# Retention plus low-rank mixer on one core: the start of the kernel put in another order, for its loads, its first two batches and the first chunks of the third

## The chip, the cores and the metric

The kernel runs on one core of a Trainium2 chip. The metric is the device time of one execution in microseconds. Before the change it is 326.08 us, the median of 13 runs (325.36 to 326.92).

## The reference

Eight batches of eight heads, 576 positions, 64 features to a head. Retention comes first, then a mixer over positions of rank 32, then a two-layer perceptron with a residual:

```python
scores = scale * np.matmul(q, k.transpose(0, 1, 3, 2))
ret = scores * Dmat[None]                 # gamma_h ** (row - col), 0 above the diagonal
x = np.matmul(ret, v)                     # heads side by side: x is (8, 576, 512)
h = x.transpose(0, 2, 1) @ U @ V          # U (576, 32), V (32, 576)
u = x + h.transpose(0, 2, 1)
out = u + np.maximum(u @ w_ch1, 0.0) @ w_ch2     # 512 -> 2048 -> 512
```

Inputs and output are float32 in HBM; the kernel multiplies in bfloat16.

## The kernel before

**Two kinds of attention.** The batches go in pairs. For batches 2 to 7 the rows of a pair are nine chunks of 128 (`order`, L576): four of the even batch, one that holds the last 64 rows of one batch and the first 64 of the other, four of the odd batch. A chunk is loaded from q, k and v (`load`, L235, three tiles of 256 KB), cast and scaled to bf16 (`cast_chunk`, L254: the aligned half of k and all of q on ACT in L261 and L264, the rest of k on DVE in L263, v on GpSimd in L272), and transposed by a DMA on SyncE's queue (`xbar`, L276). `prep` is cast and transpose. `section` (L387) then makes scores, the running state and the result on TensorE; its first matmuls (L296) need the transposed chunk.

Batches 0 and 1 are done by a start written out by hand. Their rows are four units of 256 rows (numbers 0 and 1 in batch 0, 2 and 3 in batch 1) and two half chunks J (0: the last 64 rows of batch 0; 1: the first 64 of batch 1). A unit is loaded as six tiles (`load_u`, L605, issued in L617: k, q and v in two halves of heads each), scaled or cast on GpSimd (`scale_u`, L637; `cast_u`, L630), transposed on TensorE against an identity (`T_u`, L646, copies in L664 to L669), scored (`SC_u`, L675), masked on DVE (`mask_u`, L690), multiplied by v (`RV_u`, L701) and by the state before it (`QS_u`, L744), summed into the state (`ST_u`, L760, put in bf16 by `Sblk`, L770), and scaled into x (`XS_u`, L752). The half chunks have the same steps with a J in the name; `cast_J` (L799) casts k and q, `prep_vJ` (L814) scales v on GpSimd. `warm` (L205) issues matmuls on the identity whose result nobody reads.

**Mixer and perceptron.** `mixer_items` (L417) gives MA (x times U), MH (times V, plus x, which is u; added on DVE in L464) and MT (u transposed: on TensorE with a copy on ACT in L489 for the first pair, by DMA for the others). `y1_items` (L504) is the first layer, sixteen times four matmuls (L515) and a Relu on ACT (L520) for each stretch of columns; the second half of the first pair is split into 384 and 256 columns. `y2_items` (L531) is the second layer (L549) and the store. PSUM has three buffers of the tag "big"; the Y1 results, the T_u transposes and the Y2 sums take turns in them, so each waits for the copy out of the tile three places before.

**What sets the order.** Each engine works through its instructions in the order of the program, and there is no scheduler (`tc.manual_schedule()`). `startup` (L909) does batch 0 up to the first transposed u; `first_stretch` (L1033) interleaves batch 1 with the sixteen Y1 items of batch 0 (`y(n)` emits the next n), then both mixers of the pair and the first Y1 stretches of batch 1 (`Y1(f, seg)`). `merge` (L20) then lays the rest of Y1 and Y2 against the sections of batch 2 at given fractions of the work, with `fetch(n)` (load) and `ready(n)` (prep) of chunk n of the pair at others. Later batches have the same merge with other lists.

**Loads.** q, k and v come on SyncE's queue, with the DMA transposes; U and V too (`load_u_rows`, L177). The weights come on GpSimd's queue with a cast to bf16: w1 in pieces of columns (`load_w1`, L212, of which f counts blocks of 128 columns), w2 in eight pieces of two row blocks (`load_w2`, L217). A load's issue waits in its queue until its buffer has been read; the staging pool has fifteen buffers (L70), used in turn. Unit 3's loads have a gate: GpSimd writes one element of the tile first (L615), so the issue waits for GpSimd to get there. The first w2 load waits likewise for a DVE write (L1089).

## Time and profile before

| what | value |
|---|---|
| median of 13 runs | 326.08 us |
| the profiled execution | 326.03 us, span 324.3 us |
| TensorE matmul busy | 311.2 us (96%) |
| ACT, DVE, GpSimd busy | 146.0, 172.0, 101.3 us |
| first Y1 matmul (L515) | 24.47 us |
| first Y2 matmul (L549) | 73.70 us |
| last matmul's end | 321.3 us |
| granted TensorE clock | 1.0 all along |
| loads of q, k, v in full tiles | 4.8 to 5.5 us from issue to landing (median) |
| w1 and w2 pieces of 256 KB | 8.4 us (median of 14) |

A timeline row gives the start and the length in us, engine, line, operation, what it writes and reads, the shape, how many instructions were merged, and in brackets the idle time of the engine before the row with what ended it. A q behind an engine's name (SPq) is its sequencer: it issues a transfer. The DMA share is the mean busy share of sixteen DMA engines; transfers overlap in them, so that it can go over 1. Durations of single matmuls hold the pipe's latency; from start to start a 512-column matmul takes 0.216 us.

### The profile page before, as it was taken

The page shows a single profiled execution, that of the slowest core. Times are in us where ns is not written, and L with a number is a line of the kernel's source. Part 1 is how long each engine was busy: PE and PEld are TensorE (multiplying, and loading weights), DVE is VectorE, ACT ScalarE, POOL GpSimd, SP SyncE. Part 2 cuts the span into 40 slices and gives each one's busy share as a digit, 9 for nine tenths or more (in the row PEclk, how much of TensorE's full clock was granted, in tenths as well). Part 3 has the DMA queues.
Part 4 walks back from the last instruction along what each step waited for, and adds up shares of the span by engine and source line. Part 5 has one row for each costly group of instructions (what it writes and reads, how often), then busy time and mean ns, then how long its engine had stood idle before and what let it go on. Part 6 is the DMA issues. An engine that isn't in the chain of part 4 may idle for free.

```text
span 324.3 us, 9118 instructions
## 1 busy us (share of the span) xinstructions
PE 311.2 (96%) x3860; PEld 171.2 (53%) x3885; DVE 172.0 (53%) x342; ACT 146.0 (45%) x334; POOL 101.3 (31%) x172
## 2 busy tenths in 40 slices
PE   7999989989999999999999999999999999999996
PEld 3575545755444444457644454457644444467544
DVE  7866546228635577456744477555844475500012
ACT  5857547892020484058800474058700572047400
POOL 7697239223113732142221523051321500010000
PEclk9999999999999999999999999999999999999999
DMA  7999999999965999969998599859998440330022
GB/s 211 257 239 260 235 191 195 205 169 144 260 167 128 240 196 202 206 138 191 189 192 174 142 185 209 212 141 158 189 212 183 107 68 3 105 107 0 2 78 84
DMA packets 152904, 53.30 MB, mean 164 GB/s; under 512 B 132032, under 2 KB 150336, under 8 KB 152864
## 3 DMA queue, kind: packets, MB, share of 16 engines
q1 hardware_dynamic: 144512, 40.40, 67.8%
q0 software_dynamic: 8352, 12.32, 15.6%
q8 instruction: 30, 0.49, 0.7%
q14 instruction: 10, 0.08, 0.1%
HBM read 36.85 MB, written 9.44 MB: 143 GB/s over the span
## 4 chain that ended last, share of the span: by engine, by line
PE 71%; DMA 5%; ACT 3%; DVE 3%; issue 2%; SPq 1%; DVEq 0%
PE ps_y L549 32%; PE ps_y L515 31%; DMA qkT<-qk 3%; PE pp L296 2%; DVE u L464 2%; DMA uT<-u 1%; ACT y L520 1%; PE pp L316 1%; PE pp L328 1%; PE ps_y L560 1%; DMA stage_t<-in_q_dram 1%; PE AB L358 1%; PE ph L458 1%; PE pa L431 1%; ACT s_sb L373 1%
## 5 line engine op out<-in xcount | busy, mean ns | idle before, releaser
L515 PE MATMUL ps_y<-uT,w_sb 128*128 128x256 bf16 (+2 forms) x768 | 133.1, 326 | 1.7 <-ACT y L520 1.0
L520 ACT ACTIVATE y<-ps_y 128x384 bf16<-128x384 f32 (+2 forms) x192 | 89.6, 491 | 96.7 <-PE ps_y L515 95.9
L549 PE MATMUL ps_y<-w_sb,y 128*128 128x512 bf16 x535 | 123.8, 379 | 2.2 <-issue 1.1
L515 PEld LDWEIGHTS <-w_sb 128*128 128x128 bf16 x768 | 72.3, 98 | 49.5 <-issue 3.3
L549 PEld LDWEIGHTS <-y 128*128 128x128 bf16 x560 | 52.6, 98 | 61.1
L272 POOL TENSOR_TENSOR vt<-stage_t,vscale 64x256 bf16<-64x256 f32 (+1 forms) x81 | 50.1, 619 | 63.0 <-DMA stage_t<-in_v_dram 45.0
L538 DVE TENSOR_TENSOR o_sb<-ps_y,u 128x512 f32<-128x512 f32 (+2 forms) x38 | 25.2, 664 | 82.4 <-PE ps_y L549 80.1
L541 POOL DMA_DIRECT2D out_dram<-o_sb x31 | 17.1, 553 | 105.4 <-DVE o_sb L538 101.6
L304 DVE TENSOR_TENSOR ret<-pp,triH 128x512 bf16<-128x512 f32 x27 | 18.7, 691 | 24.2 <-PE pp L328 18.7
L464 DVE TENSOR_TENSOR u<-ph,xt 128x768 bf16<-128x768 f32 (+2 forms) x24 | 21.8, 950 | 5.9 <-PE ph L458 4.2
L437 ACT ACTIVATE a_sb<-pa 128x128 bf16<-128x128 f32 x8 | 2.2, 278 | 43.3 <-PE pa L431 43.3
L344 DVE TENSOR_TENSOR xt<-pp,qscale 128x512 bf16<-128x512 f32 x27 | 18.6, 689 | 4.7 <-PE pp L328 4.2
L338 DVE COPY q<-qkT 64x256 bf16<-64x256 bf16 x48 | 13.2, 275 | 14.6 <-DMA qkT<-qk 13.6
L383 DVE TENSOR_TENSOR s_sb<-AB,Af 64x256 bf16<-64x256 f32 x42 | 17.7, 422 | 2.1 <-ACT s_sb L378 1.5
L263 DVE CAST qk<-stage_t 64x256 bf16<-64x256 f32 x54 | 18.1, 335 | 1.2
L264 ACT ACTIVATE qk<-stage_t 128x512 bf16<-128x512 f32 x27 | 16.8, 621 | 0.4 <-DMA stage_t<-in_q_dram 0.4
L635 POOL CAST qk<-stage_t 128x512 bf16<-128x512 f32 x16 | 10.5, 656 | 10.5 <-DMA stage_t<-in_q_dram 5.7
L376 ACT ACTIVATE Af<-AB 128x256 f32<-128x256 f32 x24 | 9.2, 385 | 8.3 <-PE AB L358 8.1
L692 DVE TENSOR_TENSOR ret<-psc,triU 128x1024 bf16<-128x1024 f32 x8 | 9.6, 1214 | 4.2 <-PE psc L684 4.2
L296 PEld LDWEIGHTS <-qkT 64*64 64x64 bf16 x432 | 5.6, 107 | 10.7 <-issue 7.8
L261 ACT ACTIVATE qk<-stage_t 128x256 bf16<-128x256 f32 x27 | 11.0, 408 | 0.0
L296 PE MATMUL pp<-qkT 64*64 64x64 bf16 x432 | 8.6, 198 | 1.2 <-DMA qkT<-qk 1.2
(134 smaller groups left out, 219.5 us busy)
## 6 DMA issues: line engine op xcount, KB each, us to landing
stage_t<-in_k_dram SPq DMA_DIRECT2D x32, 256.0 KB, 4.8
stage_t<-in_q_dram SPq DMA_DIRECT2D x32, 256.0 KB, 5.3
stage_t<-in_v_dram SPq DMA_DIRECT2D x32, 256.0 KB, 5.5
out_dram<-o_sb POOLq DMA_DIRECT2D x31, 256.0 KB, 3.2
w_sb<-in_moe_w_ch_dram POOLq DMA_DIRECT2D x14, 256.0 KB, 8.4
stage_t<-in_k_dram SPq DMA_DIRECT2D x8, 128.0 KB, 3.6
stage_t<-in_q_dram SPq DMA_DIRECT2D x8, 128.0 KB, 3.8
stage_t<-in_v_dram SPq DMA_DIRECT2D x8, 128.0 KB, 3.8
```

Of the source, the lines that this page charges most:

```text
L263: nc.vector.tensor_copy(out=o[to, hl], in_=f[fr, hl])
L272: nc.gpsimd.tensor_tensor(out=o[to, hl], in0=f[fr, hl], in1=w[fr, hl, :, None].to_broadcast([n, NHP, D]), op=ALU.mult)
L296: nc.tensor.matmul(pp[half(m), m ^ hl, hp * D:(hp + 1) * D], qkT[half(hl), NHP + hp, half(m)], qkT[half(hl), hp, half(m ^ hl)], start=True ...
L304: nc.vector.tensor_tensor(out=ret.rearrange("p a b i -> p a (b i)").rearrange("p a (b i) -> p a b i", i=D), in0=pp[:, :, 0:NHP * D].rearra ...
L344: nc.vector.tensor_tensor(out=st["x", pr][:, i, :].rearrange("p (hp hl d) -> p hl hp d", hl=2, d=D), in0=pp[:, :, NHP * D:2 * NHP * D].rea ...
L383: nc.vector.tensor_tensor(out=S_[half(x), 1, :], in0=Bk[half(1 - x)], in1=Af[half(1 - x), now, :], op=ALU.add)
L464: nc.vector.tensor_tensor(out=st["u", par][:, i0 - base:i0 - base + n, w].rearrange("p s (c d) -> p c s d", c=2), in0=ph[k][:, :, 0:n, :], ...
L515: nc.tensor.matmul(ps[:, 0:n, :], w1_sb[:, cc, f * P:(f + 1) * P], st["uT", par][:, c0:c0 + n, cc, :], start=(cc == 0), stop=(cc == NCC - 1),)
L520: nc.scalar.activation(out=st["y1", par][:, f, c0 * P:(c0 + n) * P], in_=ps[:, 0:n, :].rearrange("p s t -> p (s t)"), func=AF.Relu)
L538: nc.vector.tensor_tensor(out=o_sb[:, 0:n], in0=ps[:, 0:n], in1=st["u", par][:, c, w], op=ALU.add)
L541: (nc.sync if last else nc.gpsimd).dma_start(out=out_flat[r0:r0 + P, w], in_=o_sb[:, 0:n])
L549: nc.tensor.matmul(ps, st["y1", par][:, f, c * P:(c + 1) * P], w2_sb[:, f, :], start=(f == 0), stop=(f == NF - 1),)
```

## The change

There are five groups of edits. They alter no arithmetic; the tiles and the loops stay.

1. **Constants.** triH and swap are made on ACT instead of DVE; four memsets of padding go behind the first transpose copy on DVE; the memset of sblk goes to the early constants.
2. **SyncE's order.** Unit 2's k comes first, then J1's k, the rows of U, J1's q, unit 2's q, J1's v, unit 2's v. Before, U and the three J1 loads came ahead of all of unit 2.
3. **Start of the first pair.** One of two `warm(3)` goes. J0's q is scaled on GpSimd instead of DVE and its k cast earlier on ACT. T_J(0) and the second state sum move ahead of RV_u(0), and unit 1's RV, QS and XS follow at once, undivided, before GpSimd's casts of J1. In `first_stretch` a y moves from between units 2 and 3 to between unit 2's two transposes.
4. **Weights.** w1(2, 4) is issued right behind w1(0, 2). At the end w1(10, 12) and w1(12, 16) take the place of w1(10, 14) and w1(14, 16), behind unit 3's k scaling and first q cast. The second half of w2 is issued behind a one-column ACT write that stands after the third narrow Y1, and behind the first chunk's v on GpSimd.
5. **Batch 2's chunks.** The first chunk's k load waits for a GpSimd write that stands between the two casts of unit 3's q. Chunks 0 and 1 are cast and transposed inside `first_stretch` (before, `ready(0)` and `ready(1)` in the merge), chunks 2 and 3 are loaded behind those transposes.

```diff
@@ early_consts
+        nc.scalar.activation(out=triH[0:HALF], in_=tri[0:HALF, 0:HALF], func=AF.Copy)
+        nc.scalar.activation(out=triH[HALF:P], in_=tri[HALF:P, HALF:P], func=AF.Copy)
+        nc.scalar.activation(out=swap[:, 0:HALF], in_=ident[:, HALF:P], func=AF.Copy)
+        nc.scalar.activation(out=swap[:, HALF:P], in_=ident[:, 0:HALF], func=AF.Copy)
...
-        nc.vector.tensor_copy(out=triH[0:HALF], in_=tri[0:HALF, 0:HALF])
...
+        nc.vector.memset(sblk, 0.0)
@@ load
-    def load(pr, i, which):
+    def load(pr, i, which, gate=None):
...
+            if gate is not None:
+                gate.memset(c["f", j][:, 0:1, 0:1], 0.0)
@@ cast_J
+            if e is None:
+                continue
@@ startup
-        load_u_rows()
...
         zero_J(1, nc.vector)
-        load_J(1, (1, 0, 2))
-        load_u(2, (1, 0, 2))
+        load_u(2, (1,))
+        load_J(1, (1,))
+        load_u_rows()
+        load_J(1, (0,))
+        load_u(2, (0,))
+        load_J(1, (2,))
+        load_u(2, (2,))
...
         cast_u(0, 2, 1, nc.gpsimd)
+        cast_J(0, None, nc.gpsimd)
         cast_u(1, 2, 0, nc.gpsimd)
+        cast_u(1, 2, 1, nc.gpsimd)
         load_w1(0, 2)
-        cast_u(1, 2, 1, nc.gpsimd)
+        load_w1(2, 4)
...
         SC_off(1, ps_o, "po")
-        warm(3)
+        cast_J(0, nc.scalar, None)
         SC_u(1, 0, ps_sc, "psc")
         mask_u(1, 0)
-        cast_J(0, nc.scalar, nc.vector)
-        SC_u(1, 1, ps_o, "po")
-        mask_u(1, 1)
-
         acc1 = pss_tile()
         ST_u(0, ALL, acc1, True)
         Sblk(acc1, 1)
+        SC_u(1, 1, ps_o, "po")
+        mask_u(1, 1)
+        acc2 = ps_big.tile([P, NHP, P], FP32, tag="big", name="pss2")
+        ST_u(0, ALL, acc2, True)
+
+        T_J(0)
         RV_u(0, 0)
         RV_u(0, 1)
         RV_off()
         XS_u(0)
-        T_J(0)
...
         SC_J(0)
         mask_J(0)
         ST_u(1, LO, acc1, False)
         Sblk(acc1, 2)
+        prep_vJ(0)
+        cast_urows()
+        RV_u(1, 0)
+        RV_u(1, 1)
+        ST_u(1, ALL, acc2, False)
+        Sblk(acc2, 3)
+        QS_u(1, 0, 1)
+        QS_u(1, 1, 2)
+        XS_u(1)
+        RV_J(0)
+        QS_J(3)
+        XS_J(0)
         cast_J(1, nc.gpsimd, nc.gpsimd)
-        load_w1(2, 4)
         prep_vJ(1)
         load_w1(4, 6)
         scale_u(2, 0, nc.gpsimd)
...
-        load_w1(10, 14)
         scale_u(3, 0, nc.gpsimd)
-        for hh in range(2):
-            cast_u(3, 0, hh, nc.gpsimd)
-        load_w1(14, 16)
+        load_w1(10, 12)
+        cast_u(3, 0, 0, nc.gpsimd)
+        load_w1(12, 16)
+        load(*order[NI], (1,), gate=nc.gpsimd)
+        cast_u(3, 0, 1, nc.gpsimd)
@@ first_stretch
             T_u(u, 1, nc.vector)
-            if last:
-                y(1)
+            y(1)
             T_u(u, 0)
...
-        for g in range(NI, NI + 4):
-            load(*order[g], (1, 0, 2) if g < NI + 3 else (1, 0))
+        load(*order[NI], (0, 2))
+        load(*order[NI + 1], (1, 0, 2))
         unit(2, (0, 1, 2), False)
-        y(2)
+        y(1)
         unit(3, (2, 3), True)
         nc.vector.memset(w2_sb[:, 0, 0:1], 0.0)
-        for f in range(0, NF, 2):
+        for f in range(0, NF // 2, 2):
             load_w2(f)
...
         y(16)
+        prep(NI)
+        load(*order[NI + 2], (1, 0, 2))
         Y1, rest = y1_items(1, by_seg=True)
...
             Y1(f, 1)
+        nc.scalar.activation(
+            out=w2_sb[:, NF // 2, 0:1], in_=ident[:, 0:1], func=AF.Copy)
+        for f in range(NF // 2, NF, 2):
+            load_w2(f)
+        prep(NI + 1)
+        load(*order[NI + 3], (1, 0))
@@ the merge for batch 2
-            [(0.04, ready(0)), (0.05, fetch(3, (2,))), (0.06, fetch(4, (1, 0))),
-             (0.12, ready(1)), (0.13, fetch(4, (2,))), (0.20, ready(2)), (0.28, ready(3)),
+            [(0.05, fetch(3, (2,))), (0.06, fetch(4, (1, 0))),
+             (0.13, fetch(4, (2,))), (0.20, ready(2)), (0.28, ready(3)),
```

## The prediction, made before the changed kernel ran

> **What bounds the kernel now.** First the engines' shares on the page.
>
> ```profile
> PE 311.2 (96%) x3860; PEld 171.2 (53%) x3885; DVE 172.0 (53%) x342; ACT 146.0 (45%) x334; POOL 101.3 (31%) x172
> ```
>
> TensorE is busy 96% of 324.3 us. Of the 13 us left, 1.4 lie before the first matmul and 2.9 behind the last. The change leaves the matmuls as they are but for three warming ones, and from 73 us on the order stays. So what it can win lies in the waits before 73 us. I took the timeline of PE next, 0 to 75 us; these rows carry a wait that the change touches.
>
> ```profile
> 27.04 1.06 PE L655 MATMUL pst<-ident,qk 128*128 128x128 bf16 x16
> 28.44 1.02 PE L515 MATMUL ps_y<-uT,w_sb 128*128 128x512 bf16 x4 [0.34 <-DVE qkT L669]
> ...
> 40.92 0.38 PE L763 MATMUL pss<-qk 64*128 64x128 bf16 x4 [0.43 <-POOL qk L635]
> 41.56 0.38 PE L763 MATMUL pss<-qk 64*128 64x128 bf16 x4 [0.26 <-POOL qk L635]
> ...
> 66.96 0.32 PE L296 MATMUL pp<-qkT 64*64 64x64 bf16 x16 [0.26 <-DMA qkT<-qk]
> ...
> 73.07 0.32 PE L296 MATMUL pp<-qkT 64*64 64x64 bf16 x16 [0.73 <-DMA qkT<-qk]
> ```
>
> At 40.9 and 41.6 PE waits for GpSimd to cast unit 3's v, which lands late; at 67.0 and 73.1 for the transposed first two chunks of batch 2. Idle time is not the whole price: a matmul in the pipe hides about 0.16 us of each wait, so from start to start the first pair costs 1.0 us, not 0.69.
>
> Third, the stretches, by the windows view. Columns: the stretch, its length, busy time of PE, PEld, DVE, ACT and POOL, clock, DMA share, GB/s.
>
> ```profile
> 2.00:15.00 13.00, 12.13 (x137) 6.05 (x137) 11.16 (x25) 9.56 (x19) 9.31 (x17) 1.00 1.14 276
> 15.00:17.00 2.00, 1.49 (x61) 1.26 (x50) 2.00 (x4) 1.02 (x3) 1.91 (x3) 1.00 0.61 121
> 17.00:25.00 8.00, 7.37 (x159) 5.87 (x157) 5.52 (x9) 4.44 (x11) 7.01 (x12) 1.00 1.19 254
> 25.00:41.00 16.00, 14.91 (x190) 8.51 (x189) 9.87 (x13) 10.51 (x22) 8.36 (x13) 1.00 1.27 246
> ```
>
> The DMA engines are full (over 1) from 2 to 41 us but for a hole at 15 to 17, where SyncE issues five small loads in a row: (1 - 0.61) x 2 = 0.8 us of transfer lost. So the front is a queue of transfers, and its order decides. Fourth, GpSimd, which works in order:
>
> ```profile
> 20.84 1.05 POOL L816 TENSOR_TENSOR vt<-stage_t,vscaleJ 128x512 bf16<-128x512 f32 x1
> 21.83 0.80 POOL L214 DMA_DIRECT2D w_sb<-in_moe_w_ch_dram  x1
> 22.65 1.07 POOL L639 TENSOR_TENSOR qk<-stage_t,vscaleU 128x512 bf16<-128x512 f32 x1
> 23.65 0.11 POOL L615 MEMSET stage_t<- 128x1 f32 x1
> 24.71 1.63 POOL L635 CAST qk<-stage_t 128x512 bf16<-128x512 f32 x2 [0.95 <-DMA stage_t<-in_q_dram]
> ```
>
> **Part 1, the start, before the first Y1 matmul (24.47).** Three L209 matmuls go (0.65 us at 0.216). SC_u(1, 0) behind them needs T_u(1, 0)'s copy, which ends at 14.1 (L665), so it moves only from 14.35 to about 14.2. More comes from the order behind it. The posJ scaling (L805, 0.92) leaves DVE for GpSimd, both masks of unit 1 run one behind the other, and RV_u(1, ...) and QS_u follow without the waits of 0.51, 0.17 and 0.34. Counted through with the rows' own durations: masks done at 17.1, XS_u(0) 18.7, mask_J 19.4, XS_u(1) 20.95 (before: the second half at 22.1), first Y1 at 23.2. That is 1.25 us earlier. The 64-wide copies and memsets moved to ACT or later in DVE lie in ACT's idle 1.72 us before L166 and in DVE's slack; nothing.
>
> **Part 2, what that meets: SyncE's new order.** The load of v of the second half chunk (call it J1's v) moves from before unit 2's k and q loads to behind them. GpSimd scales it (prep_vJ(1)) before w1(4, 6), before scale_u(2, 0), before the gate that lets unit 3's loads go. Let L be its landing. Before: issue 16.17 + 4.5 = 20.65. After it is the last of the same set of loads, and the last of that set (unit 2's second q half) landed at 18.64 + 6.8 = 25.4. I take off the 0.8 of the hole, since large loads now lie between the small ones: **L = 24.6**. From below: 20.65 plus four loads of 0.26 MB at 276 GB/s (0.95 each), less 0.8, is 23.6. From above: w1(2, 4), now issued about 2.4 us earlier, goes ahead of it. Its landing and the next w1's lie 2.4 apart (20.00 + 8.2, 21.83 + 8.8), which gives 27.0. I stay by the row of q, because the queues served by time of issue there: w1(0, 2) landed in 4.3 us, w1(2, 4), issued behind unit 2's loads, in 8.2.
>
> The Trainium skill, "DMA: Bandwidth & Descriptors", section "Queues, rings and completion order", says that each DMA engine takes turns between its queues packet by packet. By that rule w1(0, 2) and w1(2, 4) would take their turns in front of J1's v, and this step would end at the upper bound, 2.4 us later. The 8.2 us speak against even turns, and nothing else here rests on the rule.
>
> From L: 1.05 + 0.80 + 1.07 gives scale_u(2, 0) done at 27.5 (before 23.7), and gate and two casts (0.11 + 1.63) give 29.25 (before 26.3). PE's T_u(2, 1) then starts at 27.5 instead of 27.04, T_u(2, 0) at 29.25. With the y moved between them SC_u(2, 0) starts at 29.25 + 0.45 + 0.85 = 30.55. Before, 29.39 with one y fewer: 30.25 like for like. So +0.3: the start's 1.25 is spent waiting, and the wait of 0.34 at 28.44 with it. w1(6, 8), issued behind the casts, costs the y that needs it 0.2 more: **+0.5**.
>
> **Part 3, unit 3's v.** Its loads go out at 27.6 instead of 23.8, but into a queue that is still full, and with w1(10, 12) and w1(12, 16) issued only after scale_u(3, 0) and the first q cast. Before, w1(10, 14) was issued at 29.27 and landed at 40.5, beside v (40.2 and 40.8). By the rates above v lands near 39.2 and is cast by 40, when PE comes to it at 40.8: the 1.0 us goes, **-1.0**. It cannot go twice; if v is no earlier, 0. w1(12, 16) lands near 44 and is first used at 46. The bundle w1 makes no fewer bytes and one long and six short loads as before: nothing by itself. The wait of 0.45 at 46.56 on XS_u(3) stays.
>
> **Part 4, chunks turned early.** ACT casts a chunk in 0.41 + 0.52. Two casts move: one between the last Y1 of the first half and the first of the second, one behind the third narrow Y1. At 50.7 to 55.3 ACT already sets the pace (PE waited 0.18 there for L489), so the first costs half its length, +0.45, the second about +0.2: **+0.65**. From below 0, if ACT's gaps of 0.40 and 0.16 at 53 take it; above 1.8, both in full. In return the places at 60.3 and 64.8 (0.1 each) lose theirs: **-0.2**. The two transposes are issued near 53.5 and 60 instead of 60.17 and 68.47; with landings of 4.6 to 6.8 us both are long there at 67 and 73. **-0.26 -0.73**. What is late next: ACT, whose wait of 0.32 at 69.57 stays.
>
> w2 in halves: four loads at 46.8 carry f 0 to 7, wanted at 73.7; four wait for ACT's write near 57 and for the first chunk's v on GpSimd. Before, eight loads took from 46.83 to 65.1, beside four chunks; half of that is 9 us, so the second half is in by about 68, wanted at 75.4. Hidden, with 7 us to spare. The gate for the first chunk queues q of unit 3 behind it on GpSimd, but its buffer was read by 21, so it waits for nothing. Chunks 2 and 3 are now issued behind transposes 0 and 1 on SyncE; the third transpose was issued at 71.93 and landed at 76.8, used at 77.26. If PE is 1 us ahead and this transpose is not, up to 0.5 is given back; I count 0.
>
> **Sum**: 0.5 - 1.0 + 0.65 - 0.2 - 0.26 - 0.73 = -1.0 us. The profiled execution took 326.03 (span 324.3 and 1.7 around it), the median is 326.08: forecast **325.0**.
>
> **Rivals.**
> *A, slower: GpSimd waits for J1's v.* All of part 2 shifts with L one for one, and unit 3's loads, w1(6, 8) and part 3 with it, since DMA then runs empty before unit 3's loads go out. The sum turns to a loss of over 0.65 us from L = 24.6 + 1.0 + 0.65 = 26.25. At L = 26.6 it is 2.0 worse than forecast: 327.0; at the bound 27.0, 327.4. For it: the queue is full, and w1 goes ahead. Against it: the hole at 15 to 17 and the order of landings.
> *B, no change: the gains behind 46 us are taken back.* ACT costs 1.1 instead of 0.65, and the third transpose 0.4: 325.85. For it: ACT was busy 11.05 of 13 us from 52 to 65. Against it: its idle 0.27 us per pair of Y1.
> *C, more: J1's v lands at its lower bound, 23.6.* Then 1.0 less wait: 324.0; with ACT's cost at 0, 323.3. For it: 276 GB/s was reached from 2 to 15 us.
>
> The rule for the PE clock in the Trainium skill, "TensorE: Matmul & The Clock Gate", section "What's actually happening", is that an idle window of about 3.4 us halves it. The ten first L209 ran at 0.43 us each, later ones at 0.216. My gaps before T_u(2, 1), about 2 us in two pieces, stay short of it; if not, some 2 us more are lost there, an estimate from that page.
>
> **How the numbers follow.** A run of this kernel can tell about 0.2%, 0.65 us, from no change. Forecast case 0.42 (324.3 to 325.4, faster), C 0.16 (faster), B 0.20 (same), A 0.22 (slower). So faster 0.58, same 0.20, slower 0.22. The range reaches from C with ACT's cost at 0, 323.3, to A at its bound, 327.4; what lies outside is about 1 in 8.
>
> **What would show it.** In the new timeline: the first Y1 near 23.2; GpSimd idle from about 21 to 24.6 ahead of the J1 scaling (the L816 of now), named as a wait for in_v; T_u(2, 1) near 27.5; no wait for a v cast at the unit-3 state matmuls; ACT chunk casts near 52.5 and 58; no wait for qkT at the first two batch-2 chunks. The forecast is wrong at its root if GpSimd gets J1's v after 26.2, if PE waits for w1 (a release by DMA at a Y1), or if ACT's casts make PE wait over 1.1 us from 52 to 60.

## The result, and the profile after

The changed kernel is slower: 332.52 us, the median of 11 runs (328.64 to 335.71), where the kernel before, beside it on the chips, took 326.63 (48 runs, 324.81 to 328.74). The ratio is 1.0143, with a 95% interval of 1.0117 to 1.0168. A ratio here and below compares the runs that lie within 1.5% of the fastest of their kernel; medians and ranges count all runs, so the two need not agree. The profiled execution of the changed kernel took 329.62 us (span 327.9), 3.6 more than that of before; only two others of this kernel were shorter. Forecast were 325.0 and at most 327.4.

The engines' shares answer to the first line shown of before: TensorE has the same 311.2 us of work, and 3.6 us more around it.

```profile
PE 311.2 (95%) x3857; PEld 171.2 (52%) x3882; DVE 171.7 (52%) x336; ACT 147.0 (45%) x339; POOL 102.0 (31%) x174
```

The timeline of PE in the changed kernel, at the places that the forecast spoke of (lines are one or two lower than before: L654 is T_u, L762 ST_u, L295 the first products of a chunk):

```profile
19.56 0.23 PE L762 MATMUL pss<-qk 64*128 64x128 bf16 x1 [1.21 <-issue]
...
28.71 0.62 PE L654 MATMUL pst<-ident,qk 128*128 128x128 bf16 x8 [1.21 <-POOL stage_t L614]
...
37.57 0.61 PE L654 MATMUL pst<-ident,qk 128*128 128x128 bf16 x8
...
39.99 0.51 PE L654 MATMUL pst<-ident,qk 128*128 128x128 bf16 x6 [0.84 <-POOL qk L634]
...
43.89 0.38 PE L762 MATMUL pss<-qk 64*128 64x128 bf16 x4 [0.75 <-POOL qk L634]
...
48.09 0.35 PE L430 MATMUL pa<-xt,U_O 128*32 128x128 bf16 x12
...
68.96 0.32 PE L295 MATMUL pp<-qkT 64*64 64x64 bf16 x16
...
74.59 0.32 PE L295 MATMUL pp<-qkT 64*64 64x64 bf16 x16
...
80.62 0.32 PE L295 MATMUL pp<-qkT 64*64 64x64 bf16 x16 [1.77 <-DMA qkT<-qk]
```

Three rows of before that were not shown yet: the first transposes of unit 3, the first product of the second batch's mixer, and the third chunk of batch 2.

```profile
35.99 0.61 PE L655 MATMUL pst<-ident,qk 128*128 128x128 bf16 x8
...
45.76 0.35 PE L431 MATMUL pa<-xt,U_O 128*32 128x128 bf16 x12
...
77.26 0.32 PE L296 MATMUL pp<-qkT 64*64 64x64 bf16 x16
```

"Late" is the start of a row less the start of the same row of before. Read against the rows of before: the wait for unit 3's v is still there (43.89; before 41.56, so TensorE is 2.33 us late), there is a new one for unit 3's q (39.99), and a new one in the start (19.56). At the first and second chunk of batch 2 the waits of 0.26 and 0.73 are gone, so the lateness shrinks to 2.00 at 68.96 and 1.52 at 74.59. At the third chunk, where before had no wait (77.26), there is one of 1.77 and the lateness is 3.36. TensorE ends at 324.86, before at 321.27: 3.59 later. So the loss was made in two places, before 44 us and at 80 us; of the 2.33 us of the first, 1.58 are there already at 37.57.

**The front.** GpSimd's timeline, and then the window from 26 to 28 us, of the changed kernel and below it of before (columns as in the windows of the prediction: PE, PEld, DVE, ACT, POOL, clock, DMA share, GB/s):

```profile
25.59 1.22 POOL L818 TENSOR_TENSOR vt<-stage_t,vscaleJ 128x512 bf16<-128x512 f32 x1 [4.25 <-DMA stage_t<-in_v_dram]
26.76 0.81 POOL L211 DMA_DIRECT2D w_sb<-in_moe_w_ch_dram  x1
...
28.58 0.11 POOL L614 MEMSET stage_t<- 128x1 f32 x1
...
37.73 0.60 POOL L634 CAST qk<-stage_t 128x512 bf16<-128x512 f32 x1 [2.99 <-PE ps_y L514]
38.53 0.74 POOL L211 DMA_DIRECT2D w_sb<-in_moe_w_ch_dram  x1 [0.20 <-issue]
39.27 0.12 POOL L238 MEMSET stage_t<- 128x1 f32 x1
39.33 0.61 POOL L634 CAST qk<-stage_t 128x512 bf16<-128x512 f32 x1
```

```profile
26.00:28.00 2.00, 1.50 (x16) 0.60 (x13) 0.76 (x2) 1.70 (x5) 1.98 (x3) 1.00 0.09 25
```

```profile
26.00:28.00 2.00, 2.00 (x25) 1.45 (x24) 1.06 (x3) 1.71 (x6) 2.00 (x4) 1.00 1.33 251
```

GpSimd stood 4.25 us for J1's v, which landed at 25.46. Behind that wait, in its order, are a w1 piece, the key scaling that TensorE waits for at 28.71, and the gate of unit 3's loads (28.58; before 23.65). So from 26 to 28 us hardly anything is left to transfer: a DMA share of 0.09, where before had 1.33. The gap between the two q casts at 37.73 and 39.33 is the w1 issue and the new gate.

**The third chunk.** SyncE's timeline of issues (start, time of the issue itself):

```profile
60.42 3.17 SPq L278 DMA_TRANSPOSE qkT<-qk  x1
...
64.25 2.24 SPq L242 DMA_DIRECT2D stage_t<-in_q_dram  x1
66.60 4.54 SPq L242 DMA_DIRECT2D stage_t<-in_v_dram  x1
71.25 2.08 SPq L242 DMA_DIRECT2D stage_t<-in_k_dram  x2
...
76.72 1.27 SPq L278 DMA_TRANSPOSE qkT<-qk  x1
```

The same transpose in before:

```profile
71.93 1.26 SPq L279 DMA_TRANSPOSE qkT<-qk  x1
```

The third transpose goes out at 76.72; in before it went out at 71.93. Its q had landed at 62.5, and ScalarE had cast it by 70.3. What stands ahead of it are the fourth and fifth chunk's loads, and issues that take 2 to 4.5 us where many take 0.6; w2's second half is in flight from 59.9 to 72.2.

### The profile page after: what moved, and what is told of

The parts are those of the page before. It is cut to its first block, busy times and chain, and to the rows that moved or that the text cites. A ratio compares the mean times of both kernels' runs of the same rounds, so it can differ in the third digit from the quotient of the medians.

```text
span 327.9 us, 9106 instructions
## 1 busy us (share of the span) xinstructions
PE 311.2 (95%) x3857; PEld 171.2 (52%) x3882; DVE 171.7 (52%) x336; ACT 147.0 (45%) x339; POOL 102.0 (31%) x174
## 4 chain that ended last, share of the span: by engine, by line
PE 68%; DMA 8%; ACT 3%; DVE 2%; SPq 2%; issue 2%; POOL 1%; DVEq 0%; POOLq 0%; ACTq 0%
PE ps_y L548 33%; PE ps_y L514 27%; DMA qkT<-qk 3%; DMA stage_t<-in_v_dram 3%; PE pp L295 2%; DVE u L463 2%; SPq L242 1%; ACT y L519 1%; DMA uT<-u 1%; DMA stage_t<-in_k_dram 1%; PE pp L315 1%; PE ps_y L559 1%; PE pp L327 1%; PE AB L357 1%; PE pa L430 1%
## 5 line engine op out<-in xcount | busy, mean ns | idle before, releaser
L514 PEld LDWEIGHTS <-w_sb 128*128 128x128 bf16 x768 | 72.2, 98 | 49.2 <-issue 3.5
L262 DVE CAST qk<-stage_t 64x256 bf16<-64x256 f32 x54 | 19.1, 353 | 6.2 <-DMA stage_t<-in_k_dram 5.0
L337 DVE COPY q<-qkT 64x256 bf16<-64x256 bf16 x48 | 14.0, 292 | 3.4 <-DMA qkT<-qk 2.4
L634 POOL CAST qk<-stage_t 128x512 bf16<-128x512 f32 x16 | 9.7, 616 | 7.1 <-DMA stage_t<-in_v_dram 3.5
L295 PEld LDWEIGHTS <-qkT 64*64 64x64 bf16 x432 | 5.6, 107 | 11.6 <-issue 8.3
L295 PE MATMUL pp<-qkT 64*64 64x64 bf16 x432 | 8.6, 198 | 2.2 <-DMA qkT<-qk 2.2
```

The costliest lines, as they stand in the source:

```text
L262: nc.vector.tensor_copy(out=o[to, hl], in_=f[fr, hl])
L295: nc.tensor.matmul(pp[half(m), m ^ hl, hp * D:(hp + 1) * D], qkT[half(hl), NHP + hp, half(m)], qkT[half(hl), hp, half(m ^ hl)], start=True ...
L514: nc.tensor.matmul(ps[:, 0:n, :], w1_sb[:, cc, f * P:(f + 1) * P], st["uT", par][:, c0:c0 + n, cc, :], start=(cc == 0), stop=(cc == NCC - 1),)
```

## The experiments

All are edits of the changed kernel unless said otherwise; each median stands beside one of the kernel before measured with it, 326.6 to 327.6. "Theory 1" and the like are those of the expectation above each result.

**1. J1's v ahead of unit 2's q.**

```diff
         load_J(1, (0,))
+        load_J(1, (2,))
         load_u(2, (0,))
-        load_J(1, (2,))
         load_u(2, (2,))
```

> The changed kernel with one pair of loads exchanged: J1's v is issued ahead of unit 2's q. Theory 1 (the front and the third chunk add up): of the 3.6 us that the changed kernel's TensorE ends later, 1.5 to 2.3 come from GpSimd's wait for J1's v (4.25 us, until 25.46), behind which unit 3's loads stand. With the load 0.6 to 1.0 us earlier GpSimd waits 3.3 to 3.6 us, the gate of unit 3's loads falls by as much, the first product of unit 2's second score half comes 0.6 to 1.0 us earlier, and the time falls by 0.6 to 1.0 us, to about 331.5. Theory 2 (the SP queue alone): the third chunk's transpose lands when the queue of loads allows, whatever the front does; the front gains the same 0.6 to 1.0 us, but the 1.77 us wait at the third chunk's first product grows by that, and the time stays within 0.3 us of the changed kernel's.

Measured: 332.54 us (326.71 to 337.15), ratio 1.0084 (1.0039 to 1.0130). Issued two loads earlier (17.12), J1's v was still not on GpSimd before 26.50, and the wait grew to 5.44. The time was not told apart from the changed kernel's (the medians are the same, the intervals of the ratios overlap). Both theories had the front gain 0.6 to 1.0 us; neither is right about the landing. The order on SyncE's queue alone does not decide it.

**2. The scaling of J1's v behind the gate.**

```diff
-        prep_vJ(1)
         load_w1(4, 6)
         scale_u(2, 0, nc.gpsimd)
         load_u(3, (1, 0, 2), nc.gpsimd)
+        prep_vJ(1)
```

> The changed kernel with one GpSimd step moved: the scaling of J1's v comes after the load of w1's third piece, the first key scaling of unit 2 and the gate of unit 3's loads, instead of ahead of them. Theory 1: the 4.25 us wait is what costs; w1's piece goes out at about 21.5, the gate opens at about 22.6 to 23.8, unit 3's loads fill the stretch at 26 to 28 us in which the transfers ran at a share of 0.09, unit 3's v lands at or before 41 us (41.97 and 43.17 in the changed kernel), the wait of 0.75 us there goes, and the front falls by 1.5 to 2.3 us; time 330 to 331. J1's v is still scaled in time, since its product comes two steps later. Theory 2 (bandwidth: the earlier loads push J1's v and unit 2's v back instead): J1's v lands later than 26 us, TensorE waits for the product of J1's keys and values, and the front falls by under 0.5 us. If the third chunk's transpose does not move with the front, the time is that of the changed kernel within 0.3 us although the front is earlier.

Measured: 330.32 us (328.36 to 333.22), ratio 1.0125 (1.0082 to 1.0167). The gate opened at 24.09, the DMA share from 26 to 28 us was 1.22 instead of 0.09, unit 3's v made nobody wait, and the second mixer's first product came at 46.63 instead of 48.09, although TensorE now stood 1.96 us for J1's v and ran at half clock for about 3.4 us behind it. The product that needs J1's v came at 27.42, 0.32 later than in the changed kernel, so the gain was made behind it and not in the start. So the blocking is a cause of the front's loss. The third chunk's wait grew from 1.77 to 2.37 and took part of it back.

**3. Both q casts of unit 3 together.**

```diff
+        cast_u(3, 0, 1, nc.gpsimd)
         load_w1(12, 16)
         load(*order[NI], (1,), gate=nc.gpsimd)
-        cast_u(3, 0, 1, nc.gpsimd)
```

> The changed kernel with both casts of unit 3's queries ahead of the last w1 load and of the gate of the third batch's first chunk. Theory 1: the 0.84 us wait of TensorE for the query transposes of unit 3 (at 39.99) came from GpSimd's 0.74 us issue and the gate between the two casts; it goes, and the front falls by 0.8 us less what the following wait for unit 3's v (0.75 us, a landing) takes back, so 0 to 0.8. Rival: that wait is the landing of the query's second half, and nothing moves. Time 331.7 to 332.5 by the first, 332.5 by the second.

Measured: 333.30 us (331.11 to 337.08), ratio 1.0191 (1.0148 to 1.0234). The wait in the q transposes is gone, but nothing was gained in time: in its profile TensorE stood longer before, for the J1 casts (1.47) and J1's v (0.91), and then at half clock. The wait's cause is confirmed, its worth is not measured by this run.

**4. All of w2 at once.**

```diff
-        for f in range(0, NF // 2, 2):
+        for f in range(0, NF, 2):
             load_w2(f)
...
-        nc.scalar.activation(
-            out=w2_sb[:, NF // 2, 0:1], in_=ident[:, 0:1], func=AF.Copy)
-        for f in range(NF // 2, NF, 2):
-            load_w2(f)
```

> The changed kernel with all eight w2 loads issued together after unit 3, as in the kernel before, instead of four then and four behind ScalarE's gate. Theory 1: w2's second half (issued at 59.87 to 62.79) ran beside the second chunk's transpose and the fourth chunk's loads, whose issues then took 3.2, 2.25 and 4.5 us, and so held the third chunk's transpose in the SP queue until 76.72; with w2 out of the way by about 60 us these issues take about 0.6 to 1.7 us each, the third transpose is issued by about 72 us, the wait of 1.77 us at the third chunk's first product goes, and the time falls by 1.5 to 1.8 us, to 330.7 to 331. Rival (order in the SP queue, not the collision): the third transpose stays behind the fourth and fifth chunks' loads, which wait for free buffers and for what lies eight transfers before them; the wait stays above 1 us and the time within 0.5 us.

Measured: 330.38 us (328.77 to 337.13), ratio 1.0112 (1.0070 to 1.0154). The slow issues moved to the third chunk's own loads (3.2 and 4.0 us), the third transpose was issued at 75.61, and the wait was 1.43. The rival held for the wait: with w2 away the transpose still stands in SyncE's queue behind six loads of the fifth chunk. The time fell by 2.1 us in the median, more than the rival allowed, but the intervals of the ratios overlap.

**5. The third transpose ahead of those loads.** The casts of that chunk come earlier in ScalarE's order with it.

```diff
-            [(0.05, fetch(3, (2,))), (0.06, fetch(4, (1, 0))),
-             (0.13, fetch(4, (2,))), (0.20, ready(2)), (0.28, ready(3)),
+            [(0.05, ready(2)), (0.055, fetch(3, (2,))), (0.06, fetch(4, (1, 0))),
+             (0.13, fetch(4, (2,))), (0.28, ready(3)),
```

> The changed kernel with the casts and the transpose of the third chunk put in front of the last load of the fourth chunk, instead of behind that load and the six of the fifth. Theory 1 (order in SyncE's queue): the third chunk's q had landed by about 62.5 us and its casts need 1.0 us of ScalarE, so its transpose is issued at about 67 to 69 us instead of 76.7 and lands at 72 to 76 us; the wait of 1.8 to 2.9 us at the third chunk's first product (seen in the changed kernel and in every run so far) goes, and with it a clock drop behind it where there was one. The time falls by 1.8 to 3.5 us, to 329 to 330.7. Theory 2 (transfers, not order): whatever is issued then waits for the same full queue, the transpose still lands after 79 us, and the wait stays over 1 us; the time stays within 0.5 us.

Measured: 328.91 us (327.33 to 330.78), ratio 1.0062 (1.0038 to 1.0087): a little below what theory 1 gave. The timeline of PE at the third chunk has no wait left:

```profile
78.75 0.32 PE L295 MATMUL pp<-qkT 64*64 64x64 bf16 x16
```

Issued at 68.43, the transpose's issue took 4.46 us, and it was still in time. Against the changed kernel the median is 3.6 us and the ratio 0.8% lower, with a front as late as in the changed kernel (48.76). The edit moves casts and transpose together; but in the changed kernel ScalarE was done with that chunk six us before the transpose went out, so it is the place in SyncE's queue that counts.

**6 and 7. Each part alone.** One is the changed kernel with the third batch's loads, turns and w2 as before; the other is the kernel before with only those changed.

```diff
 # third batch as before
-        load(*order[NI], (1,), gate=nc.gpsimd)
...
-        load(*order[NI], (0, 2))
-        load(*order[NI + 1], (1, 0, 2))
+        for g in range(NI, NI + 4):
+            load(*order[g], (1, 0, 2) if g < NI + 3 else (1, 0))
...
-        prep(NI)
-        load(*order[NI + 2], (1, 0, 2))
...
-        prep(NI + 1)
-        load(*order[NI + 3], (1, 0))
...
-            [(0.05, fetch(3, (2,))), (0.06, fetch(4, (1, 0))),
-             (0.13, fetch(4, (2,))), (0.20, ready(2)), (0.28, ready(3)),
+            [(0.04, ready(0)), (0.05, fetch(3, (2,))), (0.06, fetch(4, (1, 0))),
+             (0.12, ready(1)), (0.13, fetch(4, (2,))), (0.20, ready(2)), (0.28, ready(3)),
```

> The changed kernel with the third batch's loads, turns and w2 as in the kernel before: only the start, the loads' order and w1 are changed. Theory 1 (two parts that add up): no wait at the third chunk; the front is 2.3 us late at 44 us and 1.5 late at 74 us, less what the old waits for the first two transposes (0.26 and 0.73) take in, so 1 to 1.5 us slower than before where the clock stays full, and 1.7 us more for each drop of the clock to 0.5 behind GpSimd's wait (seen at 28 to 32 us in three of the four runs so far): a time of 327.6 to 330. Theory 2 (all the loss lies in the batch's part): the front's lateness is taken in by the old waits, and the time is that of before within 0.5 us.

> The kernel before with the third batch's part of the change alone: first chunk's load gated, two chunks turned early, w2 in halves. Theory 1: the front is that of before; the waits of 0.26 and 0.73 us go, and a wait of 2 to 3 us comes at the third chunk, since its transpose is issued behind the fifth chunk's loads at 74 us or later and lands at 78 to 79; with a clock drop behind it (1.7 us) in some runs. Slower than before by 1 to 2 us without, 3 with a drop: 328 to 330. Theory 2 (the batch's part is harmless where the front is on time): without the front's lateness the queue runs earlier too, the wait is under 0.7 us and the time within 0.5 us of before or faster.

Measured: without the batch's part 330.80 us (329.89 to 331.63), ratio 1.0108 (1.0077 to 1.0138); the batch's part alone 329.84 us (328.60 to 333.59), ratio 1.0092 (1.0057 to 1.0127). Each part loses about 1% alone, and together 1.4%. That the sum is less fits the third chunk: with the late front its use comes later as well, and its wait is 1.77 us in the changed kernel, 2.62 with the batch's part alone. In the first, J1's v was taken by GpSimd only at 27.43, after 6.57 us, and TensorE waited 1.91 for it; that is a worse front than in the changed kernel's profile and above what theory 1 gave. The second shows what a wait can bring with it. The timeline of PE at the third chunk and the windows around it (the last three numbers of a window are clock, DMA share and GB/s):

```profile
79.70 0.43 PE L298 MATMUL pp<-qkT 64*64 64x64 bf16 x16 [2.62 <-DMA qkT<-qk]
```

```profile
78.00:80.00 2.00, 0.30 (x23) 0.30 (x27) 0.25 (x1) 0.58 (x1) 1.23 (x2) 0.81 0.75 153
80.00:82.00 2.00, 1.67 (x63) 1.11 (x53) 1.87 (x5) 0.38 (x1) 1.18 (x2) 0.50 0.98 179
82.00:84.00 2.00, 2.00 (x9) 0.85 (x8) 1.42 (x3) 0.00 (x0) 0.00 (x0) 0.84 1.00 223
```

Behind a gap of 2.62 us the granted clock fell to 0.50 and was back at 1.00 from 84 us on: (0.19 + 0.50 + 0.16) x 2 = 1.7 us of full clock are lost, of which some 0.2 fall in the wait itself. The 16 matmuls of L298 show it, 0.43 us instead of 0.32.

**8. w1's second piece later.**

```diff
         load_w1(0, 2)
-        load_w1(2, 4)
...
         cast_J(1, nc.gpsimd, nc.gpsimd)
+        load_w1(2, 4)
         prep_vJ(1)
```

> The changed kernel with w1's second piece issued at its old place, behind the casts of J1's keys and queries (about 3 us later), and nothing else. It asks why J1's v lands at 25.5 to 26.5 us in all runs, even when it is issued ahead of unit 2's q. Theory 1 (transfers in flight share the engines): w1's second piece, in flight beside it, takes its part; with it later J1's v lands 1.5 to 2.4 us earlier, at 23.5 to 24.5, GpSimd's wait falls from 4.2 to 5.4 us to 2 to 3, and the front is 1.5 us earlier; the third chunk's wait may grow by as much. Theory 2 (served by time of issue, as forecast): w1's piece was not in its way, J1's v lands within 0.5 us of 25.5 to 26.5 and nothing moves.

Measured: 333.72 us (328.95 to 334.63), ratio 1.0137 (1.0081 to 1.0193). J1's v landed at 25.67, as theory 2 had it. Since neither 1 nor 8 brought the landing forward, either neither load is a cause or each is one by itself; the next run tells.

**9. Both loads moved** (the edits of 1 and 8, and that of 5).

> The changed kernel with both loads moved, J1's v ahead of unit 2's q and w1's second piece behind the casts of J1's keys and queries, and with the third chunk's transpose ahead of the fourth chunk's v. Each of the first two moves alone did nothing: J1's v landed at 26.4 with the first and at 25.7 with the second. Theory 1 (two causes, each enough by itself): GpSimd's pieces of w1, at 62 ns a packet and 4 us of all engines for two, starve SyncE's queue from 18 to 23 us, and unit 2's q takes its turn ahead; with both away J1's v lands at 22 to 23.5, the wait on GpSimd falls to 0 to 2 us, unit 3's loads go out by 26, the transfers no longer run empty at 26 to 28, and the front is 1.5 to 2.5 us earlier than in the changed kernel; with the third chunk's wait gone the time is 326 to 327.5. Theory 2 (another cause, the reach of SyncE's queue by what lies eight transfers before): J1's v still lands after 25 us, and the time is that of the run with the third turn alone, 328.9.

Measured: 326.90 us (325.13 to 330.70), ratio 0.9976 (0.9954 to 0.9998): theory 1. J1's v was there by 21.70, GpSimd did not wait for it at all, and the second mixer began at 44.78, 3.3 us earlier than in the changed kernel and 1.0 earlier than before (45.76). Two things had stood in its way, each enough by itself. In the packet records of the changed kernel a packet of the w1 pieces takes about 62 ns of an engine, and a 1024-packet pair of pieces so 4.0 us of all sixteen; from 19 to 20 us 186 of them ran beside 170 of SyncE's, and in experiment 1 at that time 316 beside 59. With that pair out of the way, unit 2's q loads, issued ahead and landing at 24.26 and 25.18 in experiment 8, are the next to be waited for. The third chunk is not mended by this: in the profile, which is of the longest execution (330.70), the transpose's issue took 7.67 us and TensorE waited 3.84.

**10. The batch's part alone, with the third transpose early** (kernel before, edits of 7 and 5).

> The kernel before with the third batch's part of the change, and with the third chunk's transpose ahead of the fourth chunk's v. The start stays as before. Theory 1: the batch's part lost 2.6 us at the third chunk (and up to 1.7 in a clock drop) and nothing else, and it did take away the waits of 0.26 and 0.73 for the first two transposes; with the third in time it is worth 0.7 to 1.0 us less what two casts on ScalarE cost (0.65 us wait at about 70 instead of 0.32): 326.0 to 326.7 where before has 327.0. Theory 2: the transfers of the second half of w2 make the other chunks late (v of the second or third chunk on GpSimd, the fourth chunk): the wait moves to a later chunk, and the time is 327.5 or more.

Measured: 327.37 us (324.72 to 334.82) beside 327.32, ratio 0.9988 (0.9959 to 1.0018). No gain that can be told. In its profile the transpose's issue took 7.8 us (64.67 to 72.45), and TensorE waited 1.00 and 0.72 at the third and fourth chunk: theory 2 in kind, and nearly in time (327.5 or more).

**11. The wait of 7 filled with idle matmuls.**

```diff
             c = ch[pr, n]
+            if (pr, n) == (1, 2):
+                warm(10)
             SC(c, pp)
```

> The kernel before with the third batch's part of the change, as run already (329.8 us median, 328.6 to 333.6), and ten idle matmuls (2.2 us at full clock, results unused) on TensorE just ahead of the third chunk's first product, in the wait of 2.6 us. Theory 1 (the clock): part of the loss there is the granted clock, which fell to 0.5 for about 3.4 us behind the wait; with the wait filled it stays at 1.00 in that stretch, the slow runs over 331 us do not come, and the median falls by 0.5 to 1.7 us although work was added, to 328 to 329.3. Rival: the clock has no part in it; the wait is shorter by what is filled and the time the same or, where the transpose is early, up to 1 us longer: 329.8 to 330.8 with the same spread.

Measured: 329.29 us (328.09 to 331.96), ratio 1.0065 (1.0033 to 1.0098). The windows:

```profile
78.00:80.00 2.00, 0.83 (x4) 0.20 (x2) 0.43 (x1) 0.16 (x1) 1.10 (x2) 1.00 1.10 169
80.00:82.00 2.00, 1.44 (x68) 1.05 (x70) 1.36 (x4) 0.38 (x1) 1.30 (x3) 1.00 1.12 205
```

The clock stayed at 1.00, and the mean granted clock was at least 0.999 in all eight of its runs, while it was so in two of eight without the filling. That the wait causes the drop is shown. What it costs is less well told: the median fell by 0.55 us, the intervals overlap, and the wait left behind the filling was still 1.58.

**12. Both loads moved, and the gate free** (edits of 1, 2, 5, and 8).

> The same kernel as the one with both loads moved and the third chunk's transpose early, and besides with the scaling of J1's v behind the gate of unit 3's loads on GpSimd. Theory 1: if J1's v lands by 23.5 this changes little (unit 3's loads go out about 1 us earlier, at 24 to 25; time within 0.5 us of the run without it, 326 to 327.5). If J1's v still lands after 25 us (theory 2), TensorE waits for it (1.96 us in the run with this order alone), but the transfers do not run empty at 26 to 28 us, and the time is 0.5 to 1.5 us below the run without it.

Measured: 326.26 us (324.93 to 330.21), ratio 0.9984 (0.9957 to 1.0011). GpSimd's timeline and a window of this kernel:

```profile
23.64 0.12 POOL L614 MEMSET stage_t<- 128x1 f32 x1
23.69 1.05 POOL L818 TENSOR_TENSOR vt<-stage_t,vscaleJ 128x512 bf16<-128x512 f32 x1
```

```profile
26.00:28.00 2.00, 1.49 (x16) 0.95 (x14) 1.12 (x3) 1.69 (x6) 2.00 (x4) 1.00 1.33 238
```

The gate opens at 23.64, as in before (23.65), GpSimd waits for nothing here, the DMA share stays over 1, and TensorE waits for neither q nor v of unit 3. The later w1 piece has a price: a Y1 at 28.22 waits 0.73 us for w1. Waits of 1.01 and 0.32 remain at the third and fourth chunk.

**13. The mended start alone** (12, with the third batch as before).

> The changed kernel with the third batch's loads, turns and w2 as in the kernel before, and with the start mended: J1's v ahead of unit 2's q, w1's second piece behind the casts of J1's keys and queries, the gate of unit 3's loads ahead of the scaling of J1's v. With the third batch's part as before but the start not mended it took 330.8. Theory 1 (all of the start's loss came from the late landing of J1's v): it does not come, the mixer of the second batch begins at 45 to 45.7 (46.4 before), and the front's gain of 0.7 to 1.5 us is passed on as far as the old transposes of the first chunks allow, whose waits (0.26 and 0.73 before) grow by up to as much: 326.0 to 327.3, against 327.3 of before, no clock drop at 28 to 34 us. Theory 2 (the start costs elsewhere too): 328 or more.

Measured: 327.33 us (326.33 to 330.16) beside 326.63, ratio 1.0026 (1.0000 to 1.0052); not mended it was 1.0108. So about 0.8% of the start's loss goes with the late J1's v and what stood behind it. But the gain over before that theory 1 hoped for did not come either: the second mixer began at 45.77, as early as before (45.76) with a stall of 1.83 us in the start (see part 1 below).

**14 to 17. Looking for a place for the third turn** (all with the start of 12). 14: w2 at once, third turn as in 5. 15: w2 six loads and two, third turn as in 5. 16: w2 at once, the turn six ScalarE results later. 17: two more. The edit shown is that from 14 to 17; 16 has 0.12, 0.125, 0.126 and 0.13.

```diff
-            [(0.05, ready(2)), (0.055, fetch(3, (2,))), (0.06, fetch(4, (1, 0))),
-             (0.13, fetch(4, (2,))), (0.28, ready(3)),
+            [(0.155, ready(2)), (0.156, fetch(3, (2,))), (0.157, fetch(4, (1, 0))),
+             (0.158, fetch(4, (2,))), (0.28, ready(3)),
```

> The kernel with both loads moved, the free gate and the third chunk's transpose early (326.3 us median, 324.9 to 330.2), with all eight loads of w2 at once after unit 3. Theory 1 (w2's second half, in flight at 57 to 71 us, holds the transposes): with w2 done by about 62 us the issue of the third chunk's transpose takes about 1.3 to 3 us instead of 6 to 8, it lands before 74, the wait of 1.0 us (3.8 in the slow profile of its sister) at the third chunk is under 0.3, and the time falls by 0.5 to 1 us, with fewer runs over 328. Rival (the chunks' own loads, in flight with it, do that): the issue still takes over 5 us and the wait stays; or the first two transposes, now behind eight loads of w2, become the ones that are late (waits of 0.5 us or more at the first and second chunk), and the time is the same or up to 1 us longer.

> The kernel with both loads moved, the free gate and the third turn early (326.3 us median, 324.9 to 330.2, waits of 1.0 and 0.3 us at the third and fourth chunk), with w2 as six loads at once and two behind ScalarE's gate instead of four and four. Theory 1 (w2's second half holds the third transpose): with half as much behind the gate the transpose's issue takes 2 to 4 us instead of 6 to 8, the waits at the third and fourth chunk fall from 1.3 to under 0.5 us, and the first two turns are delayed by less than they have to spare: 325.3 to 326.3. Theory 2 (as with all eight, the chunks' own loads behind the first part land later): ScalarE stands at the third chunk's casts at 61 us for 2 us or more, and the time is 328 or more.

> The kernel with both loads moved, the free gate, and w2 at once (331.9 us, with a wait of 5.6 us at 61 us), with the third chunk's casts and transpose six ScalarE results later, about 4.5 us, and ahead of the fourth chunk's v and the fifth chunk in SyncE's queue as they were. Theory 1 (the loss there was ScalarE standing at casts whose data had not landed): the third chunk's k and q land at about 64.5 to 65.7, when ScalarE now comes to them; the wait falls from 5.6 us to under 1, the transpose is issued at about 67 and lands by 73, before its use at 75 to 76; time 325.5 to 327. Theory 2 (the loss moves once more): the first and second chunks' casts and transposes, behind eight loads of w2, or the fourth and fifth chunk, are late by 1 us or more, and the time is 327.5 or more.

> The kernel with both loads moved, the free gate, w2 at once and the third chunk's turn six ScalarE results later (327.0 us median, a wait of 2.4 us at 65 us with the clock at 0.5 behind it), with that turn another two results (1.5 us) later. Theory 1: ScalarE comes to the casts at about 66.3, when the chunk's q lands (66.5), so the wait is under 0.6 us and no clock drop follows; the transpose is issued at 67 to 69 as before, lands by 74, and the time is 325 to 326.3, below both kernels. Theory 2 (the loads are what limits, and a later place makes the transpose late instead): a wait of over 1 us appears at the third to fifth chunk, and the time is 326.7 or more.

Measured: 14: 331.86 us (330.43 to 332.52), ratio 1.0145 (1.0106 to 1.0183). 15: 329.22 (326.13 to 333.18), 1.0023 (0.9994 to 1.0051). 16: 326.99 (325.40 to 331.75), 0.9973 (0.9951 to 0.9995). 17: 325.21 (324.47 to 326.65), **0.9960 (0.9937 to 0.9982)**, faster than both kernels. The chain from 14 to 17 is one of a wait that moves. With w2 away the third transpose is quick (issue 2.1 us) and TensorE does not wait for it, but the third chunk's k and q land later, and ScalarE, in whose order the casts stand, blocks everything behind them. ScalarE's and TensorE's timelines in 14:

```profile
64.50 0.42 ACT L260 ACTIVATE qk<-stage_t 128x256 bf16<-128x256 f32 x1 [4.70 <-DMA stage_t<-in_k_dram]
```

```profile
66.77 1.65 PE L514 MATMUL ps_y<-uT,w_sb 128*128 128x256 bf16 x6 [5.64 <-ACT y L519]
```

In 15 that wait was 1.85 (and the stall of the start 1.89, with half clock behind it), in 16 it was 2.39 with half clock behind it, in 17 still 1.81, more than expected, without a drop. But in 17 it is the only long one left from 50 to 90 us: the first three chunks follow without a wait.

```profile
67.64 0.60 PE L514 MATMUL ps_y<-uT,w_sb 128*128 128x256 bf16 x4 [1.81 <-ACT y L519]
68.17 0.32 PE L295 MATMUL pp<-qkT 64*64 64x64 bf16 x16
...
73.00 0.32 PE L295 MATMUL pp<-qkT 64*64 64x64 bf16 x16
...
77.19 0.32 PE L295 MATMUL pp<-qkT 64*64 64x64 bf16 x16
```

So the parts of the change in another order (the small load of J1's v early, w1's second piece late, nothing that may wait ahead of a gate, w2 at once, the third turn later) came out 0.4% below the kernel before. This is the best of several orders tried and was measured with twelve executions; in its profile, of one of its longer ones (326.14), TensorE ends at 321.38, before at 321.27.

## Why the prediction was wrong

How late TensorE was forecast to be and was, in the profiles (us, less is earlier):

| at | forecast | measured |
|---|---|---|
| first Y1 | -1.25 | +0.17 |
| unit 3's first transposes (part 2) | +0.5 | +1.58 |
| the second batch's mixer (part 3) | -0.5 | +2.33 |
| second chunk of batch 2 (part 4) | -1.0 | +1.52 |
| third chunk of batch 2 | -1.0 | +3.36 |
| the last matmul | -1.0 | +3.59 |

**Part 1 (first Y1 at 23.2, 1.25 us earlier).** It came at 24.64. The mechanism was sound where nothing cut in: 22.94 to 23.35 in experiments 2, 5, 8 and 14. Two things cut in. One was not in the forecast at all: the stall of 1.21 us at 19.56, for which the profile names no wait. In the packet records the block of instructions that is loaded next (one packet of 16 KB on the instruction queue, 1.2 us) starts at 14.1 to 15.2 us in six profiles with this start and at 16.5 to 17.5 in nine; the nine, this one among them, are exactly those with the stall (0.66 to 1.89 us). With the old start it began at 14.1 to 14.7 in all four profiles, without a stall. That the late block is the cause fits all nineteen but was not tried, and why it comes late is open. The other: where the stall is absent, GpSimd's cast of J1's q can be late instead (1.47 in experiment 3, 0.91 in 16).

**Part 2 (+0.5; L = 24.6, from the row of unit 2's q less 0.8).** This step failed first. L was 25.46 in the profile, and GpSimd took J1's v at 25.6 to 27.4 in all eight profiles with the changed start in which one or none of the two loads was moved. I took off 0.8 us for a hole in the transfers and added nothing for w1's second piece, since "the queues served by time of issue". The runs show that it was served first: J1's v comes early (by 21.70 in 9, at 21.98 in 12, at 22.46 in 13) only when both that piece and unit 2's q are behind it. The rule in the Trainium skill that I set aside ("DMA: Bandwidth & Descriptors", "Queues, rings and completion order") said that queues take turns packet by packet; the 186 beside 170 packets of experiment 9's account agree with it better than my row, the 316 beside 59 do not. Two single microseconds do not settle which rule holds.

What followed from L was priced about right up to there: T_u(2, 1) came at 28.71, 1.21 behind the forecast, with L 0.86 behind it and 0.3 more on GpSimd (it took the tile 0.13 after the landing, and the scaling 1.22 instead of 1.05). I had this mechanism as rival A: unit 3's loads behind GpSimd's wait. The step that failed with it is that rival A carried the 1.0 us of part 3 through unchanged, one for one, and so turned to a loss only at L = 26.25. At 25.46 the front was already 2.33 us late. With the gate no longer behind J1's v and J1's v early (12) all of it is back (45.50, before 45.76).

**Part 3 (-1.0, the waits for unit 3's v go).** They did not: loads issued at 28.7 instead of 27.6 landed at 41.97 and 43.17, not near 39.2. Measured at this part is +0.75 instead of -1.0. I wrote that the loads come "into a queue that is still full"; it was empty, a DMA share of 0.09 for 2 us. The text also noted that the new gate queues unit 3's q behind it, and costed only the gate, not the w1 issue of 0.74 us that now stands between the two casts: another 0.84 (39.99). In 12, where the loads went out at 23.8, both waits are gone, so the step's direction was right under a condition that the change itself broke.

**Part 4.** ScalarE's two casts were put at 0.65, less 0.2 for the places they left; TensorE shows no new wait behind either, and the wait of 0.32 at 69.57 became 0.65: 0.33 in all, so near. The waits of 0.26 and 0.73 did go, as forecast. The third transpose, "up to 0.5 given back; I count 0", is the second failed step: it gave 1.84 more lateness, with a wait of 1.77, in the profile, and a wait of 2.62 with the batch's part alone. I had seen that two chunks' loads now come behind the first two transposes on SyncE, and priced the third by TensorE's being early rather than by what is then issued ahead of it. "Hidden, with 7 us to spare" was true of w2 itself, which TensorE never waited for, and beside the point: it was in flight while SyncE issued, and those issues took up to 4.5 us. It is not what alone made them long, since with w2 at once (4) others took 3.2 and 4.0.

**The clock.** The forecast took gaps of about 2 us in two pieces to be safe, by the Trainium skill's page "TensorE: Matmul & The Clock Gate", section "What's actually happening". The runs differ: half clock followed a gap of 2.62 us in 7, and gaps of 0.91 and 1.46 with 0.4 us of work between them in 3. It did not follow the 1.77 of the changed kernel's profile, nor one of 2.9 at the third chunk of 3. Nor did it follow 1.57 and 1.46 in a row in 5, while a gap of 1.70 in 1 and one of 1.96 in 2 were followed by it. So a gap well below 3.4 us can bring it and need not. Each stretch of half clock before the last matmul is 3.41 us long, or 6.83 behind the gaps of 5.06, 3.84 and 5.64 in 8, 9 and 14; 3.41 us lose 1.7 of full clock, which agrees with the 2 us that the forecast named as an estimate. The forecast's sum had nothing for it. Of the nine executions of the changed kernel that its ratio counts, four at full clock took 329.8 us in the mean and five below it 332.2; that goes with the step from the profile's +3.6 us to the +4.7 of the ratio, though one of the four at full clock took 331.7. Why one execution drops and another does not is not settled.

**The signs.** None of the three signs that the forecast named for being wrong at its root came in the profile: GpSimd had J1's v before 26.2, no Y1 waited for w1, and ScalarE's casts did not hold TensorE. The loss came through the late landing, through the gain of part 3 that fell away with it, and through a step that was counted at nothing.

## What to carry to other kernels

A load that is moved back is not late by its place in its own queue alone. Here what another queue sent meanwhile and the loads still ahead of it each held it by itself, so undoing one of them showed nothing (1, 8) and undoing both showed it all (9). In an engine that works in order, look at what stands behind the instruction that may wait, above all a gate that lets loads go: here the transfers ran empty for 2 us behind it. A gain that depends on loads going out in time is no gain in a case where they go out late. And cost the waits in front of TensorE at more than their length when they come near 2 us, for the clock may go with them.

## What the runs showed that was not expected

- A block of instructions comes as a DMA packet of 16 KB, of 1.2 us. In the nine profiles in which it started about 2 us later, TensorE stood 0.7 to 1.9 us at the same instruction; with the old start nothing of the kind was in any of four profiles. That one causes the other was not tried.
- A w1 packet with its cast takes 62 ns of an engine, a 512-byte packet of q, k and v about 30. Two w1 pieces are 4.0 us of all engines.
- An issue on SyncE, often of 0.6 us, took 2 to 8 us at times when other loads were in flight, and all that is behind it waits. At the third chunk it was the standing behind such issues, not the transfer of the transpose, that decided; what makes an issue long was not tried by itself.
